# Attention scores of the first four pairs of heads as float32 products on the two halves of TensorE's rows, with a new set of planner constants

## The chip, the cores and the metric

The kernel runs on one core of one Trainium2 chip. The metric is the device time of one execution in microseconds (us): of the kernel before, 1377.9 us as the median of 3 runs (1376.15 to 1383.55). The core has five engines with a queue each, in which instructions start in the order in which they stand: TensorE (PE, with its weight loads as PEld), VectorE (DVE), ScalarE (ACT), GpSimd (POOL) and SyncE (SP), which here only issues DMA transfers. An instruction that has to wait for another engine or a transfer holds up all that stands behind it on its engine.

## The reference

Two stages: an attention that keeps only scores within `tau` of the row's largest, and a gated linear unit over all its outputs.

```python
# q, k, v: (8 batches, 8 heads, 576 tokens, 64); tau = 0.02
scores = scale * np.matmul(q, k.transpose(0, 1, 3, 2))
thresh = np.max(scores, axis=-1, keepdims=True) - tau
scores = np.where(scores >= thresh, scores, -1000000000.0)
scores = scores - np.max(scores, axis=-1, keepdims=True)
attn = np.exp(scores)
attn = attn / (np.sum(attn, axis=-1, keepdims=True) + 1e-09)
x = np.matmul(attn, v)                 # then as (4608 tokens, 512)
# w_gate, w_val: (512, 1536), w_out: (1536, 512)
gate = 1.0 / (1.0 + np.exp(-(x @ w_gate)))
val = x @ w_val
out = gate * val @ w_out
```

Inputs are float32 (the weights arrive in a 64-bit form that the kernel narrows itself). The kernel works in float32 throughout: either as a true float32 product on TensorE, or as three products of a high and a low part (`F32R`).

## The kernel before, in words

**Visits.** Attention goes pair of heads by pair of heads: a *visit* is one batch `b` and one pair `hp` (32 visits, names like `s_3_121`: here pair 3, head 1, tiles 2 and 3, the second of them). With 576 query rows a head has four tiles of 128 rows and 64 rows left over; the leftovers of both heads make one tile together (`s_l`, `p_l`, `tp_l`), so a visit has 9 tiles. For a tile:

- PE makes the scores `s` (128 x 576, in two halves of 288 columns, one PSUM bank each; L609). There are two `s` buffers.
- DVE takes the row maximum (`st`, L616), and DVE or POOL works out the threshold (L625); ACT makes the exponentials `p` (L630); DVE masks and sums them (L633).
- For a group of two tiles DVE takes the reciprocal of the sums (L665) and POOL scales `p` by it (L667). PE transposes `p` (`tp`, L678, and the last 64 keys `lk`, L691); ACT copies the result out of PSUM (`pt`, L640), and `pl` is copied by ACT or DVE (L640, L641). PE multiplies by V (`av`, L714), ACT copies that to `xf`.

**Two ways to the scores.** Visits of the first `NPS` = 4 pairs are *plain*: K and Q are loaded as they are, Q is scaled by ACT, and PE multiplies true float32 (`plain_scores`, L554). Both heads of a pair lie on the 128 partitions, 64 each; so that a tile of one head meets only its own half of K, the host has set the other head's half of `q0` to zero. A float32 matmul shows as two matmul records in the trace. All other visits split K and Q into high and low parts (`split_scores`, L515) and copy them between partition halves by DMA (`kd`, `qd`).

**Conversions.** The 36 weight tiles are narrowed on the chip as the attention starts (`convert`, L402): a load (`wr`), three DVE operations (L442, L446, L452), two of POOL (L429, and the low part L470) and two of ACT, then a write back to DRAM (`wid`, `wod`). `LO_DVE` names those whose low part DVE makes (L466) instead of POOL.

**The unit behind it.** A batch's products with the weights (`m`, L774, and `o`, L817) can start when its four visits are done. Six of the batches are done in pairs at the end (`two_blocks`, matmuls at L1016 and L1081) by a scheme with seven products for eight, whose sums of weights POOL makes earlier (`sums`, L862).

**What sets the order.** No order is written out. Each operation is handed to `Plan` with an engine, an estimated cost, a key and what it reads and writes. `Plan.run` (L119) plays the program through with these costs, gives each free engine the ready operation of smallest key, and emits in the order of that play. `LAG` is the delay that it assumes between an operation and one that waits for it on the named engine. `THR_UNTIL` and `LK_UNTIL` say up to which visit (by the number of its first tile) the threshold goes to POOL and the `lk` copy to ACT; later ones go to DVE. `SUM_KEY` is the key of the sums of weights, `AHEAD_TWO` how many steps ahead the weights of the paired batches are loaded.

Of the kernel before, what the change touches and what calls it, by code (L numbers as in the profile page):

```python
# [10 lines left out]
F32 = mybir.dt.float32  # L11
# [221 lines left out]
THR_FIRST, THR_UNTIL, LK_UNTIL = "POOL", 72, 72  # L233
# [18 lines left out]
DVE_LO_IN, DVE_LO_OUT = (), range(0,12,4)  # L252

LAG = {"PE": 0.4, "DVE": 0.2, "ACT": 0.2, "POOL": 0.2, "SP": 0.08}
# [8 lines left out]
SUMS_IN, SUMS_OUT, SUM_KEY = {1: (0,), 2: (1,)}, {0: (0,), 1: (1,)}, 400  # L263

AWAY = 2
AHEAD_TWO = 7
# [5 lines left out]
def act(n):  # L272
    return 0.19 + 0.0008 * n
# [15 lines left out]
def kernel(  # L289
# [3 lines left out]
    q0: bass.AP,  # L293
    k: bass.AP,
# [190 lines left out]
    class Visit:  # L485
# [68 lines left out]
        def plain_scores(self, key, n):  # L554
            b, hp, c0, c1 = self.b, self.hp, self.c0, self.c1
            WM = self.WM = c1 - c0
            kn = self.k1 = buf(("kn", "qn")[hp % 2], [P, SK], F32, f"kp{n}")
            op("SP", 1.2, key - 4, lambda: nc.sync.dma_start(out=kn.ap, in_=k[b, hp]), writes=[kn])
            W = 2 * WM + (2 * SL if self.with_left else 0)
            qn = self.q1 = buf("kd", [P, W], F32, f"qp{n}")  # L560

            heads = [(0,), (1,)] if n == "0_0" else [(0, 1)]
            for hs in heads:
                c = slice(hs[0] * WM, (hs[-1] + 1) * WM)
                op("SP", 0.9 * len(hs), key - 4, lambda hs=hs, c=c: nc.sync.dma_start(
                    out=qn.ap[:, c].rearrange("p (h c) -> p h c", h=len(hs)),
                    in_=q0[4 * b + hp, :, hs[0] : hs[-1] + 1, c0:c1],
                ), writes=[(qn, h) for h in hs])
            if self.with_left:
                op("SP", 0.3, key - 4, lambda: nc.sync.dma_start(out=qn.ap[:, 2 * WM :], in_=q[b, hp, :, SM:]),  # L570
                   writes=[(qn, 2)])
            if len(heads) == 1:
                op("ACT", act(W), key, lambda: nc.scalar.activation(qn.ap, qn.ap, AF.Copy, scale=scale_t[:, 0:1]), writes=[qn])
                return
            for i, c in enumerate((slice(0, WM), slice(WM, 2 * WM), slice(2 * WM, W))):
                op("ACT", act(c.stop - c.start), key, lambda c=c: nc.scalar.activation(
                    qn.ap[:, c], qn.ap[:, c], AF.Copy, scale=scale_t[:, 0:1]
                ), writes=[(qn, i)])

    def tile_steps(vis, g, i, key):  # L580
# [6 lines left out]
        k0 = SL if i == 0 else 0  # L587
        sv = lambda: s.ap[:, :, :HALF]
        cols = None if h is None else slice(qt * P - vis.c0, (qt + 1) * P - vis.c0)
        if vis.plain_s:  # L590
            at = 2 * vis.WM if h is None else h * vis.WM + cols.start
            steps = [(lambda: vis.q1.ap[:, at : at + P], lambda c: vis.k1.ap[:, c])]
            reads = [(vis.q1, 2 if h is None else h), vis.k1]
# [11 lines left out]

        def scores():
            for m, (st, mv) in enumerate(steps):
                for c in range(2):
                    nc.tensor.matmul(  # L609
                        s.ap[:, c, :HALF], st(), mv(slice(k0 + c * HALF, k0 + (c + 1) * HALF)),  # L610
                        start=m == 0, stop=m == len(steps) - 1,
                    )

        op("PE", 0.98 if vis.plain_s else len(steps) * 2 * mm(HALF), key, scores, reads=reads, writes=[s], also=[g.p])
# [605 lines left out]
_INS = ["q", "q0", "k", "v", "tau", "moe_w_gate", "moe_w_val", "moe_w_out"]  # L1220
# [3 lines left out]
def _laid_out(inputs):  # L1224
# [16 lines left out]
    first = _np.zeros((NPS, 2, d, 2, m), q.dtype)  # L1241
    pairs = q.reshape(b * h // 2, 2, d, s)
    for i in range(2):
        first[:, i, :, i] = pairs[:NPS, i, :, :m]
# [52 lines left out]
```

## Time and profile before

| | us |
|---|---|
| median of 3 runs | 1377.9 (1376.15 to 1383.55) |
| the profiled execution | 1375.02 |
| its span, first to last instruction | 1373.2 |
| PE busy | 1332.4 (97%) |
| DVE busy | 982.3 (72%) |
| ACT busy | 708.8 (52%) |
| POOL busy | 639.0 (47%) |

The profiled execution is 1.8 us longer than its span and 2.9 us under the median of the runs. A time on the page is in us from the span's start; a group's row gives the line, the engine, what is written and read, the count, the busy time and the mean of one in ns, and behind the last bar the idle time of the engine just before it with what ended it. A wait for several things is put down to the one that came last.

### The profile page before, as it was taken

To read this page: it belongs to the slowest core of one execution; us is meant where nothing else is said; L and a number is where in the kernel's file an instruction comes from. 1 tells how busy PE (TensorE), PEld (TensorE's weight loads), DVE (VectorE), ACT (ScalarE), POOL (GpSimd) and SP (SyncE) were. 2 spreads that over 40 slices of the span, in tenths; PEclk is the share of its full clock that TensorE was granted. 3 is DMA by queue.
4 is the path that set the end of the run, shared out by engine and by line. 5 is a ranking of instruction groups with operands and counts; after the bars stand their busy time and mean duration, and the time that the engine had idled before them with its cause. 6 is when DMAs were issued, how large, how long until landed. Compare 5 with 4: busy or idle time off the path is not lost.

```text
span 1373.2 us, 23632 instructions
## 1 busy us (share of the span) xinstructions
PE 1332.4 (97%) x8276; PEld 1099.7 (80%) x8276; DVE 982.3 (72%) x2070; ACT 708.8 (52%) x1225; POOL 639.0 (47%) x681
## 2 busy tenths in 40 slices
PE   6888999999999999999999999999999999999998
PEld 5666888888788788888888887888888888888887
DVE  5898888777778787777878783456974569745584
ACT  5776766665566666566667663222532225322242
POOL 4888865884676685686787653011000110001100
PEclk9899999999999999999999999999999999999999
DMA  5769899888688779798879677766686566766664
GB/s 214 284 218 326 286 256 272 266 242 255 206 238 245 200 226 285 203 297 246 238 221 275 208 210 260 234 184 193 208 288 215 185 194 209 245 194 187 195 208 140
DMA packets 140292, 317.70 MB, mean 231 GB/s; under 512 B 22032, under 2 KB 49168, under 8 KB 140176
## 3 DMA queue, kind: packets, MB, share of 16 engines
q1 hardware_dynamic: 140032, 316.20, 75.0%
q8 instruction: 67, 1.10, 0.3%
q14 instruction: 49, 0.40, 0.1%
q10 hardware_dynamic: 144, 0.00, 0.0%
HBM read 210.24 MB, written 54.53 MB: 193 GB/s over the span
## 4 chain that ended last, share of the span: by engine, by line
PE 88%; DMA 4%; DVE 3%; issue 2%; POOL 2%; ACT 1%; SPq 0%; POOLq 0%; ACTq 0%; DVEq 0%
PE m L774 13%; PE qb L1016 11%; PE av L714 11%; PE s L609 10%; PE tp L678 7%; PE qc L1016 7%; PE qa L1016 7%; PE o L817 6%; PE rb L1081 5%; PE rc L1081 4%; PE ra L1081 4%; PE s_l L609 2%; DVE p L633 1%; PE tp_l L678 1%; PE lk L691 1%
## 5 line engine op out<-in xcount | busy, mean ns | idle before, releaser
L667 POOL TENSOR_SCALAR p<-p,zero_t,sm 128x576 f32<-128x576 f32 x256 | 215.1, 850 | 101.6 <-DVE sm L665 61.7
L616 DVE TENSOR_REDUCE st<-s 128x1 f32<-128x576 f32 x256 | 192.8, 754 | 84.0 <-PE s L609 82.6
L630 ACT ACTIVATE p<-s,st 128x576 f32<-128x576 f32 x256 | 190.5, 748 | 66.8 <-DVE st L616 56.3
L633 DVE SCALAR_TENSOR_TENSOR p<-s,st,p 128x576 f32<-128x576 f32 x256 | 206.4, 811 | 25.2 <-ACT p L630 19.0
L929 POOL TENSOR_TENSOR gA<-gA 128x512 f32<-128x512 f32 x18 | 24.2, 1343 | 417.1 <-DVE gA L995 417.1
L640 ACT COPY pt<-tp 128x512 f32<-128x512 f32 x256 | 148.6, 587 | 74.4 <-PE tp L678 73.4
L678 PE MATMUL tp<-ident,p 128*128 128x128 f32 x1024 | 157.0, 278 | 8.4 <-POOL p L667 8.1
L609 PE MATMUL s<-kd,qd 128*128 128x288 f32 x896 | 161.6, 305 | 3.5 <-DMA qd<-q 2.4
L774 PE MATMUL m<-x,wi 128*128 128x512 f32 x576 | 161.5, 405 | 0.0
L678 PEld LDWEIGHTS tp<-ident,p 128*128 128x128 f32 x1024 | 123.3, 142 | 34.6 <-POOL p L667 13.2
L609 PEld LDWEIGHTS s<-kd,qd 128*128 128x128 f32 x896 | 133.8, 189 | 14.4 <-DMA qd<-q 2.9
L714 PE MATMUL av<-pt,vs 128*64 128x256 f32 x1024 | 126.3, 385 | 0.7 <-ACT pt L640 0.7
L817 PE MATMUL o<-g,wo 128*128 128x512 f32 x432 | 120.1, 404 | 0.0
L953 DVE TENSOR_TENSOR qu<-qb,qp 128x512 f32<-128x512 f32 x72 | 49.8, 692 | 92.2 <-PE qb L1016 66.1
L774 PEld LDWEIGHTS m<-x,wi 128*128 128x128 f32 x576 | 98.8, 189 | 13.6
L1016 PE MATMUL qa<-xs_p,wa 128*128 128x512 f32 x432 | 109.6, 389 | 0.0
L714 PEld LDWEIGHTS av<-pt,vs 128*64 128x64 f32 x1024 | 68.4, 136 | 48.5 <-issue 7.7
L1016 PEld LDWEIGHTS qa<-xs_p,wa 128*128 128x128 f32 x432 | 81.1, 188 | 16.8
L817 PEld LDWEIGHTS o<-g,wo 128*128 128x128 f32 x432 | 74.5, 189 | 10.5
L921 ACT CAST gs_p<-gA 128x512 fp32r<-128x512 f32 x54 | 32.7, 620 | 77.4 <-DVE gA L995 41.5
L991 ACT ACTIVATE gA<-qa 128x512 f32<-128x512 f32 x18 | 10.8, 598 | 103.4 <-PE qa L1016 103.4
L640 ACT COPY xf<-av 128x256 f32<-128x256 f32 x64 | 25.6, 399 | 74.1 <-PE av L714 70.7
(151 smaller groups left out, 2687.5 us busy)
## 6 DMA issues: line engine op xcount, KB each, us to landing
kd<-k SPq DMA_DIRECT2D x112, 320.0 KB, 4.9
wi<-wid SPq DMA_DIRECT2D x48, 512.0 KB, 7.4
wo<-wod SPq DMA_DIRECT2D x36, 512.0 KB, 6.9
wa<-wid SPq DMA_DIRECT2D x36, 512.0 KB, 3.3
ws<-sid SPq DMA_DIRECT2D x36, 512.0 KB, 4.4
wt<-sid SPq DMA_DIRECT2D x36, 512.0 KB, 3.3
wo_p<-sod SPq DMA_DIRECT2D x36, 512.0 KB, 4.5
qd<-q SPq DMA_DIRECT2D x112, 128.0 KB, 3.4
```

The lines of the kernel that those rows point to most:

```text
L609: nc.tensor.matmul(s.ap[:, c, :HALF], st(), mv(slice(k0 + c * HALF, k0 + (c + 1) * HALF)), start=m == 0, stop=m == len(steps) - 1,)
L616: op("DVE", 0.76, key, lambda: nc.vector.tensor_reduce(out=st.ap[:, 0:1], in_=sv(), axis=AX.XY, op=ALU.max, negate=True), reads=[s], write ...
L630: op("ACT", 0.74, key, lambda: nc.scalar.activation(p(), sv(), AF.Exp, bias=st.ap[:, 0:1], scale=1.0), reads=[s, (st, 0)], writes=[(g.p, i)])
L633: op("DVE", 0.9, key, lambda: nc.vector.scalar_tensor_tensor(out=p(), in0=sv(), scalar=st.ap[:, 1:2], in1=p(), op0=ALU.is_ge, op1=ALU.mult ...
L640: return op("ACT", act(n), key, lambda: nc.scalar.copy(dst(), src.ap), reads=[src], writes=[part])
L667: op("POOL", 0.9, key, lambda i=i: nc.gpsimd.tensor_scalar(out=p.ap[:, i * S : (i + 1) * S], in0=p.ap[:, i * S : (i + 1) * S], scalar1=zer ...
L678: nc.tensor.matmul(tp.ap[:, c, :], self.p.ap[:, o + c * P : o + (c + 1) * P], ident, is_transpose=True, start=c == 0, stop=c == NJ - 1, sk ...
L714: nc.tensor.matmul(av.ap[h * D : (h + 1) * D, a:z], vis.vs.ap[:, j, h], m(h), start=i == 0, stop=i == len(ms) - 1, skip_group_check=True,)
L774: nc.tensor.matmul(m.ap, wv[:, a, c * P : (c + 1) * P], xs[c].ap[:, z, c0:c1], start=e == 0, stop=e == 11,)
L817: nc.tensor.matmul(acc.ap, wv[:, f, a], g[fg * ND + f].ap[:, z], start=(fg, f, a, z) == (0, 0, 0, 0), stop=(fg, f, a, z) == (NFG - 1, ND - ...
L1016: nc.tensor.matmul(acc.ap, wv[:, y, (2 * h + c) * P : (2 * h + c + 1) * P], xt[prod][c].get()[:, z], start=e == 0 and prod in FIRST, stop= ...
L1081: nc.tensor.matmul(acc.ap, w.ap[:, e, c, y], gt[prod][2 * g + c].get()[:, z], start=m == 0 and g == 0 and prod in FIRST, stop=m == 5 and g ...
```

## The change

Two things are changed.

*The plain scores.* The host lays out Q of the first four pairs so that the 64 rows of a head stand twice, on partitions 0 to 63 and 64 to 127, and K so that the first half of a tile's keys stands on partitions 0 to 63 and the second on 64 to 127 (`k0`, one 128 x 352 piece for a head). The scores of a tile are then still two float32 matmuls, one per half of the keys, but each contracts over 64 rows only: one on the upper half of TensorE's rows and one on the lower. The leftover tile of both heads takes four of 64 x 64. The pieces of K are kept in the buffers of `qd` (three) instead of `kn` and `qn` (one each).

*The planner's constants.* `THR_UNTIL` 72 to 36, `LK_UNTIL` 72 to 300, the low parts of the weight tiles 18 to 23 and of three of `w_out` on DVE, `LAG` for all engines but SP, `SUM_KEY`, `AHEAD_TWO`, and the cost of a plain tile (0.98 to 0.8).

```diff
-THR_FIRST, THR_UNTIL, LK_UNTIL = "POOL", 72, 72
+THR_FIRST, THR_UNTIL, LK_UNTIL = "POOL", 36, 300
...
-DVE_LO_IN, DVE_LO_OUT = (), range(0,12,4)
-
-LAG = {"PE": 0.4, "DVE": 0.2, "ACT": 0.2, "POOL": 0.2, "SP": 0.08}
+DVE_LO_IN, DVE_LO_OUT = range(18,24), range(6,12,2)
+
+LAG = {"PE": 1.2, "DVE": 0.3, "ACT": 0.08, "POOL": 0.3, "SP": 0.08}
...
-SUMS_IN, SUMS_OUT, SUM_KEY = {1: (0,), 2: (1,)}, {0: (0,), 1: (1,)}, 400
+SUMS_IN, SUMS_OUT, SUM_KEY = {1: (0,), 2: (1,)}, {0: (0,), 1: (1,)}, 1000
...
-AHEAD_TWO = 7
+AHEAD_TWO = 8
...
+            pair = 4 * self.b + self.hp
+            self.k1 = [buf("qd", [P, HALF + SL], F32, f"kp{n}_{h}") for h in range(2)]
+            qn = self.q1 = buf("kd", [P, 2, S], F32, f"qp{n}")
+
+            for hs in [(0,), (1,)] if n == "0_0" else [(0, 1)]:
+                h = slice(hs[0], hs[-1] + 1)
+                for x in hs:
+                    op("SP", 0.7, key - 4 + x, lambda x=x: nc.sync.dma_start(out=self.k1[x].ap, in_=k0[pair, :, x]),
+                       writes=[self.k1[x]])
+                op("SP", 1.05 * len(hs), key - 4, lambda h=h: nc.sync.dma_start(out=qn.ap[:, h], in_=q0[pair, :, h]),
+                   writes=[(qn, x) for x in hs])
+            for h in range(2):
+                op("ACT", act(S), key + h, lambda h=h: nc.scalar.activation(
+                    qn.ap[:, h], qn.ap[:, h], AF.Copy, scale=scale_t[:, 0:1]
+                ), writes=[(qn, h)])
...
         if vis.plain_s:
-            at = 2 * vis.WM if h is None else h * vis.WM + cols.start
-            steps = [(lambda: vis.q1.ap[:, at : at + P], lambda c: vis.k1.ap[:, c])]
-            reads = [(vis.q1, 2 if h is None else h), vis.k1]
+
+            heads = [(0, SM, 0, SL), (1, SM, SL, P)] if h is None else [(h, qt * P, 0, P)]
+            reads = [y for x, *_ in heads for y in ((vis.q1, x), vis.k1[x])]
...
+        def plain_scores():
+            for (x, c0, r0, r1), c in itertools.product(heads, range(2)):
+                rows = slice(c * D, (c + 1) * D)
+                nc.tensor.matmul(
+                    s.ap[r0:r1, c, :HALF], vis.q1.ap[rows, x, c0 : c0 + r1 - r0],
+                    vis.k1[x].ap[rows, kc : kc + HALF], start=True, stop=True, skip_group_check=True,
+                )
+
...
-        op("PE", 0.98 if vis.plain_s else len(steps) * 2 * mm(HALF), key, scores, reads=reads, writes=[s], also=[g.p])
+        op("PE", 0.8 if vis.plain_s else len(steps) * 2 * mm(HALF), key, plain_scores if vis.plain_s else scores, reads=reads, writes=[s], also=[g.p])
```

Since the constants feed the planner, the order of all five queues changes. In the changed kernel lines behind the new argument are one higher (L609 becomes L610, L633 L634 and so on), and the plain scores have a line of their own, L602.

On DVE, at the end of the last plain visit, before the change. (`p_3_12` with `st_3_121` is that visit's last masked tile; `wb`, `wa` are conversions; `q_0` is the low part of the fifth visit's Q.)

```order
L633 SCALAR_TENSOR_TENSOR p_3_12_1231,sm_3_12_1247<-s_3_121_1233,st_3_121_1258,p_3_12_1231 128x576
L665 RECIPROCAL sm_3_12_1247<-sm_3_12_1247 128x2
L442 TENSOR_SCALAR wb_0_1303<-wa_0_1265 128x512
L446 SCALAR_TENSOR_TENSOR wb_0_1303<-wr_0_1218,wb_0_1303 128x512
L452 SCALAR_TENSOR_TENSOR wa_0_1265<-wr_0_1218,wb_0_1303 128x512
L442 TENSOR_SCALAR wb_1_1322<-wa_1_1294 128x512
L446 SCALAR_TENSOR_TENSOR wb_1_1322<-wr_1_1225,wb_1_1322 128x512
L452 SCALAR_TENSOR_TENSOR wa_1_1294<-wr_1_1225,wb_1_1322 128x512
L536 SCALAR_TENSOR_TENSOR q_0_1306<-qn_0_1244,scale_t,q_0_1306 128x640
```

The same place after the change:

```order
L634 SCALAR_TENSOR_TENSOR p_3_12_1227,sm_3_12_1272<-s_3_121_1240,st_3_121_1253,p_3_12_1227 128x576
L666 RECIPROCAL sm_3_12_1272<-sm_3_12_1272 128x2
L447 SCALAR_TENSOR_TENSOR wb_0_1265<-wr_0_1149,wb_0_1265 128x512
L453 SCALAR_TENSOR_TENSOR wb_0_1265<-wr_0_1149,wb_0_1265 128x512
L537 SCALAR_TENSOR_TENSOR q_0_395<-qn_0_219,scale_t,q_0_395 128x640
L467 TENSOR_TENSOR ws_0_1310<-wb_0_1265,ws_0_1310 128x512
```

Up to and with the first row shown, DVE has 20 L442, 20 L446 and 20 L452 in its queue before, and 19, 18 and 18 (under their new numbers) after; the tiles' own rows, 36 maxima and 36 masks, are the same. Between that row and the fifth visit's Q stand seven instructions before and three after.

On PE, the same place, where the first batch's products with the weights begin, before:

```order
L691 MATMUL lk_3_12_1334<-ident,p_3_12_1231 128x128
L714 MATMUL av_3_12_1346<-pt_3_02_1220,vs_3_538 64x256 x8
L714 MATMUL av_3_12_1346<-pl_3_02_1229,vs_3_538 64x128 x4
L714 MATMUL av_3_12_1346<-pt_3_l_1159,vs_3_538 64x64 x8
L714 MATMUL av_3_12_1346<-pl_3_l_1169,vs_3_538 64x64 x2
L609 MATMUL s_0_l_1383<-k_0_991,q_0_1306 128x288 x6
L774 MATMUL m_0_0_0_1408<-x_0_554,ws_0_359 128x512 x3
L774 MATMUL m_0_0_0_1408<-x_1_834,ws_0_359 128x512 x3
L774 MATMUL m_0_0_0_1408<-x_2_1132,ws_0_359 128x512 x3
L774 MATMUL m_0_0_0_1408<-x_3_1393,ws_0_359 128x512
L609 MATMUL s_0_000_1429<-kd_0_0_1066,qd_0_0_1313 128x288 x4
```

and after:

```order
L692 MATMUL lk_3_12_1336<-ident,p_3_12_1227 128x128
L610 MATMUL s_0_l_1339<-k_0_359,q_0_395 128x288 x6
L715 MATMUL av_3_12_1360<-pt_3_02_1235,vs_3_570 64x256 x8
L715 MATMUL av_3_12_1360<-pl_3_02_1250,vs_3_570 64x128 x4
L715 MATMUL av_3_12_1360<-pt_3_l_1168,vs_3_570 64x64 x8
L715 MATMUL av_3_12_1360<-pl_3_l_1178,vs_3_570 64x64 x2
L610 MATMUL s_0_000_1399<-kd_0_0_678,qd_0_0_965 128x288 x4
L610 MATMUL s_0_001_1412<-kd_0_0_678,qd_0_0_965 128x288 x4
L775 MATMUL m_0_0_0_1441<-x_0_579,ws_0_319 128x512 x3
```

Before, ten weight products stand ahead of the fifth visit's first scores from `kd` and `qd`; after, two tiles of these scores stand ahead of all weight products.

More of the change, by code (lines that the diff above doesn't have):

```diff
@@ L293 @@
     q0: bass.AP,
+    k0: bass.AP,
     k: bass.AP,
@@ L554, in plain_scores @@
         def plain_scores(self, key, n):
[L555 to L578, printed above, removed]
+            pair = 4 * self.b + self.hp
@@ L586, in tile_steps @@
         s = buf("s", [P, 2, SM], F32, f"s{n}")
-        k0 = SL if i == 0 else 0
+        kc = SL if i == 0 else 0
         sv = lambda: s.ap[:, :, :HALF]
@@ L609, in scores @@
                     nc.tensor.matmul(
-                        s.ap[:, c, :HALF], st(), mv(slice(k0 + c * HALF, k0 + (c + 1) * HALF)),
+                        s.ap[:, c, :HALF], st(), mv(slice(kc + c * HALF, kc + (c + 1) * HALF)),
                         start=m == 0, stop=m == len(steps) - 1,
                     )
-        op("PE", 0.98 if vis.plain_s else len(steps) * 2 * mm(HALF), key, scores, reads=reads, writes=[s], also=[g.p])
+        op("PE", 0.8 if vis.plain_s else len(steps) * 2 * mm(HALF), key, plain_scores if vis.plain_s else scores, reads=reads, writes=[s], also=[g.p])
         st = buf("st", [P, 2], F32, f"st{n}")
@@ L1217 @@
     plan.run()
-_INS = ["q", "q0", "k", "v", "tau", "moe_w_gate", "moe_w_val", "moe_w_out"]
+_INS = ["q", "q0", "k0", "k", "v", "tau", "moe_w_gate", "moe_w_val", "moe_w_out"]
 _OUTS = [((512, 4608), "float32")]
@@ L1240, in _laid_out @@
     given["q"] = _np.concatenate([q[..., :m], left.reshape(b, h // 2, 2 * d, -1)], axis=3)
[L1241 to L1244, printed above, removed]
-    given["q0"] = first.reshape(NPS, 2 * d, 2, m)
-    given["k"] = _np.concatenate([k[..., m:], k], axis=3)
+    q0 = q.reshape(b * h // 2, 2, d, s)[:NPS].transpose(0, 2, 1, 3)
+    given["q0"] = _np.concatenate([q0, q0], axis=1)
+    k = given["k"] = _np.concatenate([k[..., m:], k], axis=3)
+    k0 = k.reshape(b * h // 2, 2, d, -1)[:NPS].transpose(0, 2, 1, 3)
+    given["k0"] = _np.concatenate([k0[..., : s // 2 + s - m], k0[..., s // 2 :]], axis=1)
     v = v.reshape(b, h // 2, 2, s, d).transpose(0, 1, 3, 2, 4)
```

## The prediction

> **What bounds the kernel now.** I read the page first, then the busy times by stage. The share of PE over the whole span says that PE bounds; the stages say where it doesn't.
>
> ```profile
> span 1373.2 us, 23632 instructions
> PE 1332.4 (97%) x8276; PEld 1099.7 (80%) x8276; DVE 982.3 (72%) x2070; ACT 708.8 (52%) x1225; POOL 639.0 (47%) x681
> 6.00:130.00 124.00, 97.39 (x605) 70.13 (x606) 102.89 (x203) 87.87 (x162) 91.57 (x124) 0.94 0.75 261
> 10.70:116.00 105.30, 84.84 (x521) 60.66 (x521) 92.95 (x189) 76.65 (x143) 79.51 (x113) 0.94 0.73 252
> 280.00:420.00 140.00, 136.02 (x1025) 114.32 (x1026) 104.69 (x269) 86.97 (x148) 95.55 (x100) 1.00 0.85 243
> 826.00:1000.00 174.00, 174.00 (x820) 143.13 (x819) 103.50 (x156) 56.03 (x98) 26.16 (x19) 1.00 0.66 216
> ```
>
> The columns of a stage are its length and then the busy time of PE, PEld, DVE, ACT and POOL. From 130 us on PE hardly rests, and from 826 on not at all: there a time can only fall if PE gets less to do, and this change takes no work from it there. In the first 130 us, the four plain visits, PE is idle for 26.6 us of 124, and DVE is the fullest: 92.95 of 105.3 us between its first maximum and its last plain mask. So every us by which the plain visits end earlier moves the whole rest forward by one. What DVE waits for in its remaining 12.3 us, and what PE waits for in both stages:
>
> ```profile
> DVE st L616 <- PE s L609: 12.0, 13, 4.9
> DVE st_l L616 <- PE s_l L609: 2.7, 3, 1.3
> ...
> PE s L609 <- DVE p L633: 14.3, 9, 2.6
> ...
> PE tp L678 <- POOL p L667: 6.6, 5, 2.2
> PE s L609 <- DVE p L633: 1.1, 1, 1.1
> PE lk L691 <- ACT pt L640: 0.3, 1, 0.3
> ```
>
> The first two rows are DVE between 10.7 and 116 us (total, times, longest); the longest, 4.9, is the one before the very first maximum and lies ahead of that stretch, so 12.0 + 2.7 - 4.9 = 9.8 us of scores waited for remain in it. The third is PE from 6 to 130 us: it waits for a score buffer to be masked, DVE for scores: the two hand a ring of two buffers to and fro, with conversions on DVE as filler. The last three rows are all that PE waits for from 130 to 826 us, 8.0 us.
>
> **The plain scores.** What they cost now, and what a pair of half products in this kernel costs, stands in one piece of PE's queue:
>
> ```profile
> 37.07 1.95 PE L714 MATMUL av<-pt,vs 128*64 128x256 f32 x16
> 38.85 0.61 PE L714 MATMUL av<-pl,vs 128*64 128x128 f32 x8
> 39.39 1.09 PE L678 MATMUL tp<-ident,p 128*128 128x128 f32 x8
> ...
> 40.43 1.14 PE L609 MATMUL s_l<-kp,qp 128*128 128x288 f32 x4
> 41.40 1.13 PE L609 MATMUL s<-kp,qp 128*128 128x288 f32 x4
> 42.46 0.87 PE L714 MATMUL av<-pt,vs 128*64 128x256 f32 x6
> ```
>
> A plain tile is four records and takes 41.40 - 40.43 = 0.97 us, 0.243 a record, or 0.84 ns a column. The products with V are float32 too, but each uses half of TensorE's columns, two heads side by side: 16 records in 38.85 - 37.07 = 1.78 us, 0.111 a record, 0.43 ns a column. Two halves therefore run at the same time, if the halves are of columns. Halves of rows occur nowhere before. Bounds for a tile: 0.49 if the halves overlap fully as those of `av` do; 0.97 if not at all. If a product's two records follow each other ahead of the second half, only the middle two overlap: 0.73. Going over to another shape costs little: 42.46 - 41.40 = 1.06 against 0.97 us, 0.09, and 39.39 - 38.85 = 0.54 for the eight short records whose four pairs at half of 0.217 make 0.43, 0.11. With about 0.1 for it I take 0.65 us a tile, 0.3 saved.
>
> The Trainium skill ("TensorEngine Tiling (Array Packing)", Key Properties) says that tiles of the array run in parallel but that changing the tiling mode drains TensorE; the transposes between scores keep the full mode, so this rule speaks against the change. The trace has the drain at the 0.09 and 0.11 us above; by the rule without the parallel part a tile would cost about 1.07.
>
> PE's own saving, 36 tiles x 0.3 = 11 us, lands in a stage in which PE has 26.6 us to spare; it counts only where DVE waits for scores. There are 15 such waits after the first. Each shrinks by one tile's saving, 0.3 us, and by twice that where the clock is halved, as it is around 58.92, where four records take twice as long:
>
> ```profile
> 58.92 2.29 PE L609 MATMUL s<-kp,qp 128*128 128x288 f32 x4 [2.06 <-DVE p L633]
> L609 PE MATMUL s<-kp,qp 128*128 128x288 f32 x128 | 43.4, 479 | 19.4 <-DVE p L633 14.3 <-ACT qp L576 3.3 <-PE lk L691 0.9
> ```
>
> 15 x 0.3 is 4.5 us, and the first maximum comes some 0.6 earlier since the first tile of all is at half clock. Bounds: nothing (the ring then waits for ACT or POOL instead), and all 9.8 plus 0.6. I take **4.6 us**.
>
> **Work that leaves the stage.** Up to the last plain mask DVE's queue holds one L442, two L446 and two L452 fewer; none of the low parts that DVE takes over comes ahead of it. By their means:
>
> ```profile
> L442 DVE TENSOR_SCALAR wb<-wa 128x512 int32<-128x512 int32 x21 | 14.4, 685 | 0.1
> L446 DVE SCALAR_TENSOR_TENSOR wb<-wr,wb 128x512 int32<-128x512 int32 x20 | 13.8, 690 | 0.3
> L452 DVE SCALAR_TENSOR_TENSOR wa<-wr,wb 128x512 int32<-128x512 int32 x20 | 13.5, 677 | 0.2
> ```
>
> 0.685 + 2 x 0.690 + 2 x 0.677 = **3.4 us**, on the engine that is full. They come back behind the stage, where DVE is 75% busy and PE's products cover them; a weight tile is needed only every 12 products.
>
> **The way into the weight products.** Now PE runs ten of them and then waits for the fifth visit's copies:
>
> ```profile
> 122.63 1.05 PE L609 MATMUL s_l<-k,q 128*128 128x288 f32 x6
> 123.52 2.44 PE L774 MATMUL m<-x,ws 128*128 128x512 f32 x10
> 128.39 0.79 PE L609 MATMUL s<-kd,qd 128*128 128x288 f32 x4 [2.43 <-DMA qd<-q]
> 114.97 0.82 DVE L633 SCALAR_TENSOR_TENSOR p<-s,st,p 128x576 f32<-128x576 f32 x1 [0.59 <-ACT p L630]
> 120.03 1.03 DVE L536 SCALAR_TENSOR_TENSOR q<-qn,scale_t,q 128x640 fp32r<-128x640 f32 x1
> 121.47 1.95 SPq L546 DMA_DIRECT2D qd<-q  x2
> ```
>
> The low part of Q is begun 4.2 us after the last mask ends (114.97 + 0.82 = 115.8), issued at 121.47 and there at 128.39, 6.9 us later. In the new order it follows after a reciprocal and two operations (0.17 + 0.69 + 0.68) and is ready 2.6 us after the mask; the copies of K for it stand far ahead in SP's queue. With the issue's 3.4 us (median of `qd`, row below) the copies are there 6.2 us after the mask, with 6.9 us 9.7. PE is done with `av` 122.63 - 115.8 = 6.8 us after it now, and the new order lets the leftover scores fill in front of that. So PE waits 0 to 2.9 us there, with nothing ahead to fill, against 2.43 now: between 2.4 gained and 0.5 lost. I take **1.2 us**.
>
> ```profile
> qd<-q SPq DMA_DIRECT2D x112, 128.0 KB, 3.4
> ```
>
> **Moved between engines, 130 to 826 us.**
>
> ```profile
> L641 DVE COPY pl<-lk 128x128 f32<-128x128 f32 x104 | 29.7, 286 | 19.0 <-PE lk L691 18.4
> L641 DVE COPY pl_l<-lk_l 128x128 f32<-128x128 f32 x26 | 7.5, 289 | 2.7 <-PE lk_l L691 2.6
> L640 ACT COPY pl<-lk x24: 264/283/290, 20.5 to 192.8; 128x128 f32<-128x128 f32 x24
> L625 DVE TENSOR_SCALAR st<-st,ntau_t 128x1 f32<-128x1 f32 x208 | 43.4, 209 | 4.2
> L625 POOL TENSOR_SCALAR st<-st,ntau_t 128x1 f32<-128x1 f32 x32 | 8.5, 268 | 16.5 <-DVE st L616 16.2
> L470 POOL TENSOR_TENSOR ws<-wa,ws 128x512 fp32r<-128x512 f32 x21 | 26.8, 1277 | 5.9 <-ACT ws L464 5.9
> ```
>
> 130 copies leave DVE: -37 us, and come to ACT at 0.283: +37. Thresholds of two visits go from POOL to DVE: 18 x 0.27 = 5 us less on POOL, 18 x 0.21 = 4 more on DVE. Six low parts more on DVE: 7.7 off POOL, some 4 on DVE. POOL loses 12.5 us, DVE about 29. The order is planned anew with an assumed 1.2 us before every PE operation that waits for another engine, so transposes and V products stand later behind more weight products. PE's waits there, 8.0 us, may all go, or as much may be added (they double). Their largest releaser is POOL, which gets less to do, so I take **2 us** gained. `SUM_KEY` and `AHEAD_TWO` touch the stage from 826 on and what feeds it; PE has no gap there to win, and loads one step earlier are covered by PE's products: I take 0. If that cover failed, each load that comes late would stall PE for a part of its way, of the size of the 3.4 us of `qd` above.
>
> **Sum.** 4.6 + 3.4 + 1.2 + 2.0 = 11.2 us off the profiled execution's 1375.0, which is 1363.8. The runs' median lies 2.9 us above that execution, so I forecast 1377.9 - 11.2 = **1366.7 us**.
>
> **Rivals.**
>
> *DVE keeps the ring's time.* DVE is 88% full, and the waits go over to ACT's exponentials or POOL's thresholds; or the halves of rows do not overlap. Then only the 3.4 us of conversions and at most 1.2 at the way out count: 1377.9 - 3.4 - 1.2 = 1373.3. For it: DVE's own work there. Against it: 9.8 us of its idle time name the scores. The same result comes from the clock: PE's stage has four stretches at half clock (10 us windows at 0.83, 0.75, 0.91 and 0.85), and PE will be idle more. Each further one of 3.4 us costs up to 1.7 us of PE's time; four more eat 6.8 of the 11 us that PE saves.
>
> ```profile
> 30.00:40.00 10.00, 8.85 (x51) 6.45 (x52) 8.89 (x18) 6.50 (x11) 8.44 (x11) 0.83 0.79 272
> 50.00:60.00 10.00, 6.15 (x19) 4.38 (x20) 8.15 (x18) 6.55 (x13) 6.49 (x10) 0.75 0.68 247
> ```
>
> The Trainium skill ("TensorE: Matmul & The Clock Gate", Part 1) has the rule behind this: an idle window of about 3.4 us halves the clock until a busy one has passed. The trace agrees: the slow stretches lie where PE was idle.
>
> *ACT becomes late, and it ends slower.* The `pl` copies now queue on ACT behind exponentials of 0.75 us, and PE's V products wait for them; there are 56 of these in the 28 split visits, and now PE waits for none of them. From 11.2 / 56 = 0.2 us of wait each the gain is gone. At one exponential each, 0.75, it would be 42 us; at half of that 1377.9 - 11.2 + 21 = 1388. Against it: ACT has (696 - 488) us to spare even with the copies.
>
> ```profile
> L630 ACT ACTIVATE p<-s,st 128x576 f32<-128x576 f32 x224 | 166.9, 748 | 57.8 <-DVE st L616 48.9 <-PE s L609 3.9 <-POOL p L667 2.0
> 700.00:826.00 126.00, 126.00 (x968) 106.27 (x968) 99.62 (x260) 82.20 (x140) 87.28 (x90) 1.00 0.77 226
> ```
>
> (ACT was busy 451 us from 130 to 826, the sum of five stages of which the last is shown; with 37 more 488.)
>
> *Everything falls into place.* The scores stop being waited for (10.4), the 8.0 us go, and 3.4 + 2.4: 24 us, 1354.
>
> **How the numbers follow.** Chances: the forecast (1360 to 1371) 0.48, DVE or the clock keeping the time (1371 to 1378) 0.27, ACT late 0.13, everything 0.12. Two in ten lie outside a range of **1356 to 1381**: its low end is near the last rival, its high end the case in which the first two terms give 4 us and the 8.0 us double (1377.9 - 4 + 8 = 1382). The likeliest case's own range is 1360 to 1371. What can't be told from no change is 0.5%, 6.9 us: 1371 to 1385. Faster than that takes the forecast, the last rival and a little of the first: 0.62; the same 0.28; slower 0.10, most of the case with ACT.
>
> **What would show it.** Records of L602 in pairs a few ns apart, and a tile at 0.5 to 0.75 us; if it still takes 0.97, the halves don't overlap. The first weight product some 8 to 10 us earlier than 123.5. DVE's wait for scores from 10.7 us to its last plain mask at 5 us or less; if it is still near 10, the ring is set by something else. PE's waits from there to the end of attention under 8 us; V products that wait for ACT would be the second rival. From the end of attention on, 547 us as before; if that stage is longer, I have missed what the sums and loads do.

## The result and the profile after

The changed kernel takes **1360.7 us** as the median of 4 runs (1358.07 to 1361.72), the kernel before 1380.4 beside it (4 runs, 1376.15 to 1383.55). The ratio is 0.9857 with a 95% interval of 0.9822 to 0.9891: between 1.1 and 1.8% faster. The forecast was 1366.7, in a range of 1356 to 1381.

The profiled execution of the changed kernel took 1360.57 us, that of the kernel before 1375.02. The two profiles differ by 14.4 us, the medians by 19.7. Over 31 more runs of the kernel before (1372.81 to 1388.14, median 1378.7) its profiled execution lies near the low end. The working below explains the 14.4; why one execution of the same program takes 1373 and another 1388 was not looked into.

First the page of the changed kernel and its busy times by stage (length, then PE, PEld, DVE, ACT and POOL with their instructions, granted PE clock, DMA share, GB/s):

```profile
span 1358.8 us, 23693 instructions
PE 1321.8 (97%) x8292; PEld 1085.6 (80%) x8292; DVE 969.0 (71%) x1964; ACT 735.7 (54%) x1357; POOL 623.0 (46%) x657
9.20:103.80 94.60, 73.17 (x518) 45.41 (x518) 88.40 (x182) 75.23 (x143) 76.81 (x110) 0.90 0.82 275
826.00:1000.00 174.00, 174.00 (x792) 144.20 (x788) 111.43 (x167) 57.42 (x100) 21.49 (x16) 1.00 0.67 221
```

DVE is busy 13.3 us less than before over the whole span and ACT 26.9 more, as copies moved from one to the other. PE still has no idle time from 826 to 1000 us (last row). The third row is the stage from the first maximum to the last plain mask. The same stage of the kernel before:

```profile
10.70:115.80 105.10, 84.64 (x519) 60.53 (x519) 92.78 (x187) 76.45 (x142) 79.31 (x113) 0.94 0.72 252
```

It fell from 105.1 to 94.6 us. PE worked 11.5 us less in it (84.64 to 73.17), DVE 4.4 less (92.78 to 88.40), and DVE's idle time halved, from 12.3 to 6.2. The granted clock went down, from 0.94 to 0.90.

What a plain tile now looks like: in the kernel before, one that PE starts after a wait (1.21 us), and the same with the tile right behind it (2.18); in the changed kernel a lone tile, a leftover tile and again two behind each other; then the four records of one tile by their line (shortest, median and longest in ns, first and last start).

```profile
24.16 1.21 PE L609 MATMUL s<-kp,qp 128*128 128x288 f32 x4 [1.72 <-DVE p L633]
24.16 2.18 PE L609 MATMUL s<-kp,qp 128*128 128x288 f32 x8 [1.72 <-DVE p L633]
```

```profile
43.21 0.76 PE L602 MATMUL s<-kp,qp 64*128 64x288 f32 x4
56.49 0.72 PE L602 MATMUL s_l<-kp,qp 64*64 64x288 f32 x8
46.84 1.50 PE L602 MATMUL s<-kp,qp 64*128 64x288 f32 x8 [0.95 <-DVE p L634]
```

```profile
L602 PE MATMUL s<-kp,qp x4: 402/440/507, 46.8 to 47.2; 64*128 64x288 f32 x4
```

The first two of the four records start within 0.02 us of each other (both between 46.83 and 46.85), where records of full rows follow each other by 0.243: two run at a time, as one from each half of the rows would. A lone tile takes 0.76 us from first start to last end where one of full rows took 1.21. From the start of one tile to the start of the next it is 1.50 - 0.76 = 0.74 us where it was 2.18 - 1.21 = 0.97.

What DVE waits for in that stage (total, times, longest), and then PE from 120 to 826 us:

```profile
DVE st L617 <- PE s L602: 5.7, 5, 4.6
DVE st_l L617 <- PE s_l L602: 1.5, 2, 1.1
DVE p_l L634 <- POOL st_l L626: 1.4, 1, 1.4
DVE p L634 <- ACT p L631: 0.9, 1, 0.9
```

```profile
PE s L610 <- DVE p L634: 2.1, 2, 1.5
PE tp L679 <- POOL p L668: 1.9, 3, 1.6
```

Without the 4.6 ahead of the first maximum DVE now waits 5.7 + 1.5 - 4.6 = 2.6 us for scores, against 9.8 before. PE's waits up to the end of attention fell from 8.0 to 4.0.

The way from the last plain mask into the weight products, first on DVE and then on PE:

```profile
103.02 0.81 DVE L634 SCALAR_TENSOR_TENSOR p<-s,st,p 128x576 f32<-128x576 f32 x1
```

```profile
103.00 3.01 PE L715 MATMUL av<-pt,vs 128*64 128x256 f32 x15 [0.16 <-ACT pt L641]
108.74 1.95 PE L715 MATMUL av<-pt,vs 128*64 128x256 f32 x16
...
113.71 0.77 PE L610 MATMUL s<-kd,qd 128*128 128x288 f32 x4 [1.29 <-DVE p_l L634]
114.32 2.88 PE L775 MATMUL m<-x,ws 128*128 128x512 f32 x12
118.81 0.76 PE L610 MATMUL s<-kd,qd 128*128 128x288 f32 x4 [1.61 <-DVE st L626]
```

The first weight product starts at 114.3 us (123.5 before), 10.5 us after the last mask ends at 103.8 (7.7 before).

The new buffers for K do something beside the halves. The plain visits no longer hold `kn` and `qn`, and the fifth visit's Q is loaded into `qn` at 12.22 us, where it came at 111.56 before (SP's queue, before and after):

```profile
111.56 0.33 SPq L525 DMA_DIRECT2D qn<-in_q_dram  x1
```

```profile
12.22 0.33 SPq L526 DMA_DIRECT2D qn<-in_q_dram  x1
```

Then the end of attention and the first product of the paired batches, before and after:

```profile
836.87 18.43 PE L817 MATMUL o<-g,wo 128*128 128x512 f32 x80
855.14 1.52 PE L1016 MATMUL qa<-xs_p,wa 128*128 128x512 f32 x6
```

```profile
826.95 13.44 PE L818 MATMUL o<-g,wo 128*128 128x512 f32 x58
840.23 1.52 PE L1017 MATMUL qa<-xs_p,wa 128*128 128x512 f32 x6
```

Attention leaves 58 products of the unit behind it instead of 80, which is order only. From the first paired product PE never waits: 1373.2 - 855.1 = 518.1 us before, 1358.8 - 840.2 = 518.6 after. So the 14.4 us come about as follows (the work on the two sides of a mark is not quite the same: two score tiles of the fifth visit now stand ahead of the first weight product):

| stretch | before | after | difference |
|---|---|---|---|
| start to first maximum | 10.7 | 9.2 | -1.5 |
| plain stage to its last mask | 105.1 | 94.6 | -10.5 |
| last mask to first weight product | 7.7 | 10.5 | +2.8 |
| to the first paired product | 731.6 | 725.9 | -5.7 |
| to the end | 518.1 | 518.6 | +0.5 |

### The profile page after: what moved, and what is told of

Read it like the earlier page. It is cut to its first block, busy times and chain, and to the rows that moved or that the text cites. A ratio compares the mean times of both kernels' runs of the same rounds, so it can differ in the third digit from the quotient of the medians.

```text
span 1358.8 us, 23693 instructions
## 1 busy us (share of the span) xinstructions
PE 1321.8 (97%) x8292; PEld 1085.6 (80%) x8292; DVE 969.0 (71%) x1964; ACT 735.7 (54%) x1357; POOL 623.0 (46%) x657
## 4 chain that ended last, share of the span: by engine, by line
PE 85%; DVE 5%; DMA 4%; POOL 2%; issue 2%; ACT 1%; SPq 1%; DVEq 0%; POOLq 0%; ACTq 0%
PE m L775 14%; PE qb L1017 11%; PE av L715 10%; PE s L610 7%; PE qc L1017 7%; PE qa L1017 7%; PE tp L679 7%; PE rb L1082 5%; PE o L818 5%; PE rc L1082 4%; PE ra L1082 4%; DVE p L634 1%; PE s_l L610 1%; DVE st L617 1%; PE lk L692 1%
## 5 line engine op out<-in xcount | busy, mean ns | idle before, releaser
L634 DVE SCALAR_TENSOR_TENSOR p<-s,st,p 128x576 f32<-128x576 f32 x256 | 205.5, 811 | 25.3 <-ACT p L631 22.4
L610 PE MATMUL s<-kd,qd 128*128 128x288 f32 x896 | 163.3, 308 | 5.0 <-DVE p L634 2.1
L775 PE MATMUL m<-x,wi 128*128 128x512 f32 x576 | 157.8, 402 | 0.0
L610 PEld LDWEIGHTS s<-kd,qd 128*128 128x128 f32 x896 | 132.1, 189 | 12.4 <-issue 5.2
L818 PE MATMUL o<-g,wo 128*128 128x512 f32 x432 | 117.0, 401 | 0.0
L775 PEld LDWEIGHTS m<-x,wi 128*128 128x128 f32 x576 | 100.1, 188 | 14.7
```

Of the source, the lines that this page charges most:

```text
L610: nc.tensor.matmul(s.ap[:, c, :HALF], st(), mv(slice(kc + c * HALF, kc + (c + 1) * HALF)), start=m == 0, stop=m == len(steps) - 1,)
L634: op("DVE", 0.9, key, lambda: nc.vector.scalar_tensor_tensor(out=p(), in0=sv(), scalar=st.ap[:, 1:2], in1=p(), op0=ALU.is_ge, op1=ALU.mult ...
L775: nc.tensor.matmul(m.ap, wv[:, a, c * P : (c + 1) * P], xs[c].ap[:, z, c0:c1], start=e == 0, stop=e == 11,)
L818: nc.tensor.matmul(acc.ap, wv[:, f, a], g[fg * ND + f].ap[:, z], start=(fg, f, a, z) == (0, 0, 0, 0), stop=(fg, f, a, z) == (NFG - 1, ND - ...
```

## The experiments

The theory to test was that of the prediction: the plain stage is PE and DVE in turn, so a shorter score tile ends it earlier, and the constants add a part of their own. The rivals: the gain is that of the constants and their order, with the halves covered by other work; and, after the first runs, the planner's delays alone against the set of constants as a whole. A third one, the new buffers of K and the lower assumed cost of a tile, goes with the halves in every variant of the changed kernel and has no run of its own. All kernels are variants of the changed kernel unless said. Medians are given with the ratio to the kernel before on the same chip (95% interval). Stage marks are of one profiled execution each, which may lie some us from the median; where it lies far, this is said.

**Each part alone.** All constants as before, halves kept:

```diff
-THR_FIRST, THR_UNTIL, LK_UNTIL = "POOL", 36, 300
+THR_FIRST, THR_UNTIL, LK_UNTIL = "POOL", 72, 72
...
```

`DVE_LO_IN`, `DVE_LO_OUT`, `LAG`, `SUM_KEY` and `AHEAD_TWO` likewise.

> The plain scores on two halves of the rows, with all of the planner's old constants (only the cost of a plain tile is the new 0.8). Theory A, the halves shorten the plain visits and the constants the stage behind them: the first weight product at 114 to 116 us instead of 123.5 (114.3 with the whole change), PE's idle time from there to the last V product still about 10 us, span 1363 to 1366. Theory B, the plain visits belong to DVE and it is the new order that shortens them: first weight product at 121 to 123, span 1370 to 1373.

Measured: 1370.3 us, 0.9919 (0.9886 to 0.9951). The stage and the way out of it:

```profile
9.10:107.50 98.40, 77.66 (x533) 48.64 (x533) 90.86 (x184) 75.98 (x144) 76.93 (x111) 0.88 0.80 271
117.74 4.71 PE L775 MATMUL m<-x,ws 128*128 128x512 f32 x20
```

The halves, with the buffers of K and the assumed cost that come with them, give 10 us without the new constants. The stage is 6.7 us shorter than before and begins 1.6 earlier. The way from the last mask to the first weight product is 10.2 us instead of 7.7, nearly the changed kernel's 10.5, so it grows without the new constants too. From there to the first paired product it takes what it took (732.0). The first weight product at 117.7 lies between the two theories.

The other way round, the kernel before with the new constants and its own full-row scores:

```diff
-LAG = {"PE": 0.4, "DVE": 0.2, "ACT": 0.2, "POOL": 0.2, "SP": 0.08}
+LAG = {"PE": 1.2, "DVE": 0.3, "ACT": 0.08, "POOL": 0.3, "SP": 0.08}
...
```

The other constants likewise, except a tile's cost.

> The new constants alone, the plain scores on all rows as before. Theory A: first weight product at 120 to 123 us, PE's idle time behind it about 6 us instead of 10.4, span 1366 to 1370. Theory B: first weight product at 114 to 117, span 1358 to 1362.

Measured: 1379.1 us over 10 runs, 0.9987 (0.9962 to 1.0012).

```profile
10.90:119.00 108.10, 83.09 (x505) 59.66 (x506) 92.92 (x187) 75.95 (x141) 77.64 (x111) 0.94 0.71 238
132.36 5.01 PE L774 MATMUL m<-x,ws 128*128 128x512 f32 x13
```

Alone the constants give nothing that can be measured, and the first weight product fits neither theory. (This profile is of an execution of 1384.5 us, 5 above its median, which by itself does not make up for 132.4.) The two parts do not add: -10 and -1 alone, -20 together. But this kernel also keeps the old buffers: the fifth visit's Q is loaded into `qn` at 115.6 us, against 12.2 in the changed kernel and 11.9 with the halves alone.

**The halves taken away in an order that stays the same.** Every queue as in the changed kernel; only the two operands of a product reach over all 128 rows. A plain score is then a sum over both halves of the keys.

```diff
-                    s.ap[r0:r1, c, :HALF], vis.q1.ap[rows, x, c0 : c0 + r1 - r0],
-                    vis.k1[x].ap[rows, kc : kc + HALF], start=True, stop=True, skip_group_check=True,
+                    s.ap[r0:r1, c, :HALF], vis.q1.ap[:, x, c0 : c0 + r1 - r0],
+                    vis.k1[x].ap[:, kc : kc + HALF], start=True, stop=True, skip_group_check=True,
```

> The whole change, every queue in the same order, but each plain product contracts over all 128 rows, so that two products of a tile cannot share TensorE. (The scores of the first four pairs are then sums over both halves and not the reference's; nothing else differs.) A tile goes from about 0.5 back to 0.97 us. Theory A: first weight product 6 to 9 us later than 114.3, span 1365 to 1368. Theory B (time is in the order, not in PE's tile): first weight product within 2 us of 114.3, span 1358 to 1361.

Measured: 1369.9 us, 0.9903 (0.9865 to 0.9941), 9.2 us above the changed kernel by the medians and 6 by the ratios, whose intervals overlap a little. (The profiled execution took 1374.0, 4 above this median.)

```profile
10.30:110.70 100.40, 80.21 (x521) 56.13 (x522) 89.22 (x182) 75.70 (x143) 77.02 (x110) 0.98 0.76 255
106.05 1.21 PE L602 MATMUL s<-kp,qp 128*128 128x288 f32 x4 [0.64 <-DVE p L634]
...
DVE st L617 <- PE s L602: 10.3, 12, 5.4
DVE st_l L617 <- PE s_l L602: 2.5, 4, 1.3
```

A tile is back at 1.21 us, DVE waits 10.3 + 2.5 - 5.4 = 7.4 us for scores instead of 2.6, and the last mask is 6.9 us later (110.7 against 103.8). That is shown, then: the pair of halves shortens DVE's wait and with it the stage. It also shows what the sum of the two parts hid. The same new constants with full-row products cost 1379.1 in the order made for them and 1369.9 in the order, and with the buffers of K, that belong to the halves. Between a third and a half of the 20 us is the faster product (6 to 9 us). The rest comes with full rows too: it is the order that the new constants give together with the new buffers and the lower assumed cost of a tile. The early load of the fifth visit's Q makes the buffers the likelier of these two, but no run separates them.

**What PE's time is worth in the plain stage.** Four, and in another kernel eight, extra transposes of a constant behind each plain tile, written into columns of the score buffer that nothing reads (here with four):

```diff
+            for c in range(4):
+                nc.tensor.matmul(
+                    s.ap[:, c % 2, SM - P :], ident, ident, is_transpose=True, start=True, stop=True, skip_group_check=True
+                )
```

With four:

> The whole change, with four transposes of the identity behind each plain tile's products, into columns of its PSUM banks that nothing reads: 0.43 us of PE's time a tile, in a stage in which PE rests. With the change the clock was halved for about 20 us of the plain visits (from 23, 68, 95 and 102 us), before for 14. If the half clock costs time on the way (scores of 1.3 us instead of 0.76, V products of 3.0 instead of 2.0 just ahead of the first weight product): no half clock in the last 20 us before the first weight product, which comes 2 to 4 us before 114.3, 1356 to 1360. If it lies beside DVE's work: same first weight product within 1 us, or up to 2 later by the transposes themselves, 1360 to 1363.

With eight:

> As the kernel with four, but eight transposes a tile, 0.87 us, with which PE is as busy as with full-row products (whose clock was halved only once, 3.4 us). If four are too few to hold the clock, eight do: first weight product 1 to 3 us before 114.3. If PE's extra time hurts more than the clock helps, it comes 2 to 6 us after 114.3, as the full-row products did with 121.2.

Measured: 1375.5 us, 0.9979 (0.9956 to 1.0002), and 1388.2 us, 1.0063 (1.0043 to 1.0082). The stage with four, then with eight:

```profile
9.30:115.70 106.40, 87.86 (x662) 58.71 (x663) 90.11 (x182) 76.73 (x143) 77.46 (x110) 0.92 0.73 245
DVE st L621 <- PE s L607: 16.0, 16, 4.8
```

```profile
10.50:129.00 118.50, 97.78 (x801) 70.41 (x803) 90.63 (x182) 76.92 (x143) 77.59 (x110) 0.98 0.65 215
DVE st L621 <- PE s L607: 24.1, 25, 5.8
```

In one order, with DVE's work the same within 2.2 us, the stage follows PE's busy time:

| | PE busy | DVE idle | stage | clock |
|---|---|---|---|---|
| changed kernel | 73.2 | 6.2 | 94.6 | 0.90 |
| full rows | 80.2 | 11.2 | 100.4 | 0.98 |
| four transposes a tile | 87.9 | 16.3 | 106.4 | 0.92 |
| eight | 97.8 | 27.9 | 118.5 | 0.98 |

From the first row on, each us of PE's time costs 0.7, 0.7 and 0.9 us of DVE's idle time (5.0 of 7.0, 10.1 of 14.7, 21.7 of 24.6), although PE is idle for about a fifth of the stage. The two engines do overlap: 73.2 and 88.4 us of work fit into 94.6. But a us added to a plain tile lies mostly on the path, since DVE cannot start on a tile that isn't made. Both forecasts were missed: the first weight product came at 126.2 and 139.5 us. Eight transposes were taken to make PE as busy as full rows do, and made it busier by 17.6 us (97.8 against 80.2). They bring the clock back to 0.98, as full rows do, but cost far more than that returns.

**DVE's work ahead of the last mask.** The keys of the weight tiles' conversions run in steps of 1.5; a smaller step puts more of them into the plain stage, a larger one fewer; 1.3 is shown, the other kernel has 2.5.

```diff
-CONV_IN, CONV_OUT = (10, 1.5), (56, 3)
+CONV_IN, CONV_OUT = (10, 1.3), (56, 3)
```

With 1.3:

> The whole change, with the weight conversions asked for earlier (a key step of 1.3 tiles instead of 1.5). Up to the last plain mask DVE then has one L443, two L447, two L453, two low parts, one maximum and the low part of Q more in its queue: 0.69 + 1.38 + 1.35 + 1.36 + 0.75 + 1.1 = 6.6 us. If DVE's work ahead of that mask sets the end of the plain visits, the mask ends 5 to 7 us later than 103.8. If the ring of scores sets it and conversions only fill gaps: less than 2 us later. The total follows the first weight product if nothing is won back behind: 1363 to 1368 in the first case, 1359 to 1363 in the second.

With 2.5:

> The whole change, with the conversions asked for later (a step of 2.5). DVE has one each of L443, L447 and L453 less up to the last plain mask, 2.1 us. DVE's work sets it: the mask ends 1.5 to 2.5 us before 103.8, 1357 to 1361. The ring sets it: no difference there. If the weights of the first batch come too late, the first weight products wait for conversions and it is over 1364.

Measured: 1377.1 us, 0.9983 (0.9961 to 1.0004), and 1374.9 us, 0.9962 (0.9933 to 0.9991). The stage with step 1.3; then the stage and PE's waits from 104 to 840 us with step 2.5:

```profile
8.50:108.20 99.70, 75.98 (x545) 47.84 (x541) 95.25 (x191) 79.24 (x149) 78.96 (x113) 0.85 0.84 291
```

```profile
8.90:99.90 91.00, 70.03 (x521) 43.32 (x521) 86.86 (x179) 74.49 (x141) 74.94 (x109) 0.94 0.81 276
...
PE tp L679 <- ACT xf L641: 5.0, 2, 3.2
PE tp L679 <- POOL p L668: 3.6, 2, 2.2
PE s L610 <- DVE p_l L634: 3.4, 1, 3.4
```

DVE's work in the stage counts, as forecast: 6.9 us more of it (95.25 against 88.40) make the stage 5.1 longer, and with 1.5 less it is 3.6 shorter. The totals missed their forecasts, by 9 and 14 us. (The first profile is of an execution 3 us below its median.) The first kernel's stretch from the first weight product (120.7) to the first paired one is 732.4 us instead of 725.9. The second kernel, whose last mask is 3.9 us earlier than the changed kernel's, has its first weight product only 1.2 earlier and ends 14 us later, with 741.4 us in that stretch: PE waits 14.9 us there instead of 5.7, and is busy 6.3 us more (726.5 against 720.2), with about 12 us at half clock where the changed kernel has none. The weight products did not wait for conversions, the case that was named for over 1364. An earlier end of the plain stage is not yet an earlier end.

**The constants one by one.** Each of the next four puts one group of the changed kernel's constants back to its old value (`LAG`; `LK_UNTIL` 300 to 72; the two `DVE_LO` ranges; `SUM_KEY` with `AHEAD_TWO`), the fifth keeps the new `LAG` alone and puts all others back.

```diff
-LAG = {"PE": 1.2, "DVE": 0.3, "ACT": 0.08, "POOL": 0.3, "SP": 0.08}
+LAG = {"PE": 0.4, "DVE": 0.2, "ACT": 0.2, "POOL": 0.2, "SP": 0.08}
...
-THR_FIRST, THR_UNTIL, LK_UNTIL = "POOL", 36, 300
+THR_FIRST, THR_UNTIL, LK_UNTIL = "POOL", 36, 72
...
-DVE_LO_IN, DVE_LO_OUT = range(18,24), range(6,12,2)
+DVE_LO_IN, DVE_LO_OUT = (), range(0,12,4)
...
-AHEAD_TWO = 8
+AHEAD_TWO = 7
```

Old `LAG`:

> The whole change with the planner's old delays (LAG) only. If it is the longer assumed delay before PE that takes PE's idle time behind the first weight product from 10.4 to 5.7 us: idle time back at 9 to 11, first weight product within 1.5 us of 114.3, span 1362 to 1365. If it is the work moved off DVE and POOL: idle time 5 to 7 us, span 1358 to 1360.

Old `LK_UNTIL`:

> The whole change, with the copies of the last keys back on DVE from the seventh visit on (LK_UNTIL 72). Theory C: no more than 3 us from the whole change's 1360.7. Theory D: the 37 us that go back to DVE make PE wait, 1365 to 1370, with PE's idle time behind the first weight product at 9 us or more. The plain visits stay as they are in both: first weight product within 1 us of 114.3.

Old `DVE_LO` ranges:

> The whole change, with the low parts of weight tiles 18 to 23 back on POOL and the old three of w_out on DVE. Theory C: 1359 to 1363. Theory D: POOL's 7.7 us back at the start of the split visits make the transposes wait, 1364 to 1368.

Old `SUM_KEY` and `AHEAD_TWO`:

> The whole change, with SUM_KEY 400 and AHEAD_TWO 7. From the first product of the paired batches to the end it took 518.1 us before and 518.5 with the change, so nothing is to be had there: 518 again, and 1359 to 1363 in both theories, unless the sums' place in POOL's queue decides about the visits ahead of it: then 1364 or more, with the difference in PE's waits for POOL.

Halves and the new `LAG` only:

> The halves and the new delays (LAG), all other constants old. Halves alone took about 10 us off, the whole change about 20, the constants alone 1. Theory C, the delays are what the second 10 us hang on: 1360 to 1364, PE's idle time behind the first weight product 5 to 7 us. Theory D, the other constants are needed too (work off DVE and POOL): 1367 to 1372, idle time 9 us or more.

| kernel | median | ratio (95%) | first weight product | from there to first paired product | of which PE is idle |
|---|---|---|---|---|---|
| changed | 1360.7 | 0.9857 (0.9822 to 0.9891) | 114.3 | 725.9 | 5.7 |
| old `LAG` | 1374.8 | 0.9961 (0.9936 to 0.9987) | 115.8 | 738.9 | 15.1 |
| old `LK_UNTIL` | 1369.5 | 0.9947 (0.9924 to 0.9969) | 115.2 | 730.6 | 7.9 |
| old `DVE_LO` | 1366.6 | 0.9927 (0.9901 to 0.9954) | 114.5 | 730.4 | 6.5 |
| old `SUM_KEY`, `AHEAD_TWO` | 1361.2 | 0.9878 (0.9854 to 0.9903) | 116.4 | 725.7 | 6.1 |
| halves and new `LAG` only | 1369.5 | 0.9941 (0.9917 to 0.9964) | 113.9 | 731.7 | 9.6 |
| halves only | 1370.3 | 0.9919 (0.9886 to 0.9951) | 117.7 | 732.0 | 9.8 |

PE's waits with the old `LAG` (116 to 840 us), with the old `LK_UNTIL` (132 to 830), with the old `DVE_LO` (116 to 830), and with halves and the new `LAG` only (116 to 830):

```profile
PE tp L679 <- POOL p L668: 5.4, 5, 2.1
PE s L610 <- DVE p L634: 2.6, 1, 2.6
PE lk L692 <- ACT pt L641: 2.6, 1, 2.6
PE s L610 <- issue: 2.1, 1, 2.1
```

```profile
PE s L610 <- DVE p L634: 4.0, 3, 1.7
```

```profile
PE s L610 <- DMA qd<-q: 2.9, 1, 2.9
```

```profile
PE s L610 <- DMA qd<-q: 4.0, 1, 4.0
```

The first weight product is within 2.1 us in all these but the last row. What a group costs when put back is 14, 9, 6 and 1 us by the medians (14, 12, 10 and 3 by the ratios to the kernel before on the same chip), and the last can't be told from nothing. It lies mostly behind the first weight product. With the old `LAG` most of it is waits of PE (15.1 us against 5.7), whose releaser changes from kernel to kernel. With the old `DVE_LO` the waits hardly grow; PE is busy 3.7 us longer, with 6.8 us at half clock where the changed kernel has none, so the waits forecast for POOL's work did not come. The new delays alone add nothing to the halves. The other constants without the new delays are 4.5 us behind no new constants at all, with intervals that overlap. So the new delays don't carry the second ten us alone; several groups are needed together. The other groups were not added alone, and `THR_UNTIL` was never put back alone. Whether the work moved by `LK_UNTIL` and `DVE_LO` costs by itself, or only because every queue is laid out anew, these runs cannot tell. None of the variants beat the change.

## Why the prediction was right, and where it was not

The direction and the range held, and the sum of 11.2 us compares with 14.4 in the profiles and 19.7 in the medians. That the mark in the middle held, the first weight product "8 to 10 us earlier" (9.2), is partly luck: the stage gained 4 us more than its two terms, and the way out of it gave 4 back. Its terms:

- **Half products overlap.** Right, and the size nearly so: 0.65 us a tile from start to start was taken, 0.3 less than 0.97; it measures 0.74 between two plain tiles, 0.23 less. The lone tile, from its first start to its last end, fell by more, 0.45 (from 1.21 to 0.76). The Trainium skill ("TensorEngine Tiling (Array Packing)", Key Properties) says that tiles of the array run in parallel and that a change of mode drains it; the trace agrees with the first in two records that start within 0.02 us of each other, and the second is at most a part of the 0.76.
- **Fewer waits for scores, 4.6 us.** The mechanism was right, the term too small: DVE's idle time in the stage fell by 6.2 us and the first maximum came 1.5 earlier, 7.7 together. Of these the halves give 5.0 + 1.1 = 6.1 in one order (against full rows); the rest is the order's. The working itself, 4.5 + 0.6, makes 5.1, of which 4.6 was taken. The step that was mis-sized is "15 waits by 0.3 us". It multiplied the saving of one tile from start to start by the listed waits only. Where DVE waits for a tile that PE has just begun, what counts is the time from first start to last end, and that fell by 0.45; and the kernels in one order show 0.7 us of DVE's idle time for each us of PE's busy time, waits or not. That PE's busy time in the stage fell by 11.5 us, where the forecast said 11, is luck: between kernels of one order the halves take 7.0 off, since they also cost clock (below).
- **Conversions that leave, 3.4 us.** Agrees, with somewhat more: DVE worked 4.4 us less, and the kernel with more conversions ahead shows that such work counts, at 5.1 us of the stage for 6.9 (in an order of its own).
- **The way into the weight products, 1.2 us.** Wrong in sign. The step that failed is "PE waits 0 to 2.9 us there" for the copies of Q. They are no longer what PE waits for. Two score tiles now stand around the first weight products and wait for DVE, 1.29 and 1.61 us, together 2.9 where PE waited 2.43 before: 0.5 lost, the bad end of what the text allowed. From the last mask to the first weight product it takes 2.8 us more, partly since two score tiles have moved ahead of that mark and products with V ran at half the clock, 3.01 us against 1.95.
- **PE's waits to the end of attention, 2 us.** Right in sign and half the size: 8.0 to 4.0. The stretch from the first weight to the first paired product is 5.7 us shorter, which counts the moved tiles on the other side: from the last mask to the first paired product, this term and the one above gained 2.9 us together, where 3.2 was forecast.
- **The last stage, 0.** Right: 518.1 to 518.6 us from the first paired product. The mark in the text, the end of attention at 826 us, was badly chosen: products with V run on to 836.9 us, and weight products may stand on either side (18.4 us of them behind it before, 13.4 after).

What the sum had no place for is that its terms hang together. It priced halves and order apart, 3.4 + 1.2 + 2.0 = 6.6 us for the order. The constants without the new buffers and the tile's new cost gave 1, and not surely that; with both, and full rows, 10 or more.

The rivals. *DVE or the clock keeps the time:* the waits for scores hardly went over to ACT and POOL (DVE waits 0.9 + 1.4 us for them, 1.0 before). The clock did what that rival says: up to the first weight product the trace has 20.5 us at half clock instead of 13.7. Four windows of the changed kernel show where (the column after POOL is the clock).

```profile
20.00:30.00 10.00, 7.60 (x33) 5.05 (x34) 9.66 (x21) 9.72 (x18) 9.02 (x13) 0.66 0.66 219
70.00:80.00 10.00, 8.92 (x52) 5.45 (x52) 9.73 (x20) 7.27 (x14) 7.28 (x13) 0.78 0.62 188
90.00:100.00 10.00, 6.07 (x28) 3.41 (x26) 9.03 (x19) 7.10 (x14) 7.24 (x11) 0.83 0.92 288
100.00:110.00 10.00, 8.88 (x60) 6.48 (x62) 9.83 (x18) 7.36 (x17) 8.06 (x11) 0.83 0.81 266
```

It did not decide, but it was no small part. The same order with full rows had 3.4 us at half clock, 17 less. Were PE busy through all of these, they would be 8.5 us of its busy time, and at 0.7 us each 6 us of the stage: an estimate from above that no run tests, since the transposes that brought the clock back cost more themselves.

The forecast says that "the slow stretches lie where PE was idle". They lie right behind such places. Two windows of the changed kernel in a row:

```profile
91.51:94.92 3.41, 0.76 (x5) 0.36 (x5) 3.38 (x9) 1.86 (x3) 2.64 (x4) 1.00 0.94 281
94.92:98.33 3.41, 3.41 (x13) 2.28 (x13) 2.54 (x5) 2.24 (x4) 2.84 (x5) 0.50 1.04 354
```

In the second PE is busy throughout, at half clock; in the first it was busy for 0.76 us of 3.41. The like holds for all eight slow stretches of the two kernels up to the first weight product: in the 3.41 us before, PE was busy for 22 to 50%. The Trainium skill ("TensorE: Matmul & The Clock Gate", Part 1) lets the clock fall after an idle window of about 3.4 us. The trace agrees with the length, and shows that PE need not be idle for the whole of it: half of it was enough at times, though not each time (1.69 us of 3.41 from 20.88 us in the kernel before were not followed by half clock).

*ACT late:* in the changed kernel PE's products with V wait 1.1 us for ACT up to 130 us and not at all after that. *Everything falls into place,* 24 us and 1354: the median stayed 7 us above it.

## What to carry to other kernels

Where two engines hand a ring of two buffers to and fro, price a saving on the "idle" one by the whole time it works there (here 0.7 to 0.9 us for each us), not by the waits listed beside it; a filler in the same order measures that price directly. Watch what else a change sets free: here two buffers, and with them a load that came 99 us earlier; whoever tests the parts one by one has to test these too. When a duration changes in a program whose order is planned, fit the planner's constants anew, and judge them by the end of the program: constants that did nothing in the old kernel gave half of the gain in the new one, and a kernel whose first stage ended 3.9 us earlier ended 14 us later.

## What was not expected of the hardware

Two float32 products over 64 rows each, on the two halves of TensorE's rows, run side by side though each shows as two records: the first two records start within 0.02 us. The overlap is not full: two such tiles behind each other take 0.74 us from start to start, three quarters of the 0.97 with full rows and not half. A leftover tile of four 64 x 64 products, eight records, takes 0.72 us, as long as a whole tile (0.76).

Taking work from TensorE can slow it. In the same order the plain visits had 20.5 us at half clock with the halves and 3.4 with full rows, and a group of products with V that takes 1.95 us took 3.01. The slow stretches came right behind 3.4 us in which TensorE was busy for 22 to 50% of the time; it did not have to stand still.
